# A linear-attention and MLP block on one core: key weights transposed by DMA, layernorm woven into the key loop in a fixed order, two output stages moved up

## The chip, the cores and the metric

The kernel runs on one core of a Trainium2 chip. The metric is the device time of one execution in microseconds (us); lower is better. Times of many runs are given as medians. A ratio is the mean time of one kernel's fast runs over the mean of the other's fast runs of the same rounds, so it is not quite the ratio of the medians quoted beside it; the other kernel of a ratio is always the kernel before. Positions inside an execution (start times, waits) come from the profile of one execution, whose span is some 2 us shorter than the timed run.

In the profile, PE is TensorE (matmuls), PEld its weight loads, DVE is VectorE, ACT is ScalarE, POOL is GpSimd and SPq the queue of SyncE that issues the DMA transfers. A tile is 128 of the 2048 rows; t numbers tiles from 0 to 15. The trace also records the granted clock of TensorE, which in these traces is either full or half; a stretch at half is called cold, or a half-clock window, below.

## The reference, cut to what matters

```python
# x: 1 x 2048 x 640; 32 heads of 20
def A(x):                                    # on the layernorm of x
    q, k, v = split_heads(x @ wqkv)
    pq, pk = q @ w_phi, k @ w_phi            # per head
    phi = lambda p: concat(softmax(p), softmax(-p))
    kv = phi(pk).T @ v;  z = phi(pk).sum(0)  # per head, over all rows
    return merge(phi(pq) @ kv / (phi(pq) @ z + 1e-6)) @ wo
h   = x + A(layernorm(x))
out = h + silu(layernorm(h) @ w1) @ w2
```

The sum over all rows in kv and z cuts the program in two: every key tile must have been added to the state before the first query tile can be finished.

## The kernel before

A prologue prepares weights. wv is used as loaded; the key weights wk are loaded, transposed by TensorE (wT), copied out of PSUM and multiplied with w_phi ("fold") into Wfk. Tiles 0 to 3 of the normalised x are transposed by TensorE (xT); tiles 4 to 15 go to DRAM (xs) and come back through a DMA transpose (XnT).

```python
def ln1(ts):                       # layernorm of a list of tiles, in one batch
    ...  bn_stats, bn_aggr per tile on VectorE
    ...  rstd for all of them on GpSimd
    ...  xn = (X - mean) * rstd per tile on VectorE

def stageK(t):
    ps = proj(t, Wfk)                                    # 10 matmuls
    Ek[:, 0], Ek[:, 1] = exp(ps), exp(-ps)               # ScalarE
    nc.vector.tensor_reduce(Sk, Ek, axis=X, op=add)      # row sums
    nc.vector.reciprocal(Sk, Sk)
    nc.gpsimd.tensor_tensor(Ek, Ek, Sk, op=mult)         # the multiply
# stageC(t) adds the product of Vp(t) and the normalised Ek(t) to the state in PSUM
...
with tc.manual_schedule(engines={PE, SP}):   # the scheduler orders VectorE, ScalarE, GpSimd
    for t in range(T):
        if t in (1, 5):
            ln1([t + 7, t + 8, t + 9, t + 10])
            xT_dma(t // 4 + 2)
            ...
        stageK(t)
        if t >= 4: stageV(t)
        if t >= 3: stageC(t - 3)
        ...
# later, per query tile: stageD (product with the state, division on VectorE -> o),
# stageT (transpose o), stageG (times wo, residual, second layernorm -> hn), stageTH (transpose hn),
# then stageF1 / stageF2, the MLP, in four groups of four tiles
```

The softmax here doesn't subtract the row's maximum and nothing guards it: scores larger than these inputs give would overflow.

## Time and profile before

| kernel before | |
|---|---|
| median time | 293.71 us (15 runs, 292.78 to 294.84) |
| span of the profiled execution | 291.3 us |
| busy PE / DVE / ACT / POOL | 259.6 / 141.9 / 128.8 / 72.5 us |
| mean granted TensorE clock | 0.969 |
| stageK(0) / stageC(0) / first stageD / first F1 matmul start at | 24.85 / 41.03 / 100.01 / 130.79 us |

The starts in the table, with that of stageK(5) at 46.76, cut the execution into stretches. The views of the hole before stageC(0) stand in the prediction below. One more view matters for the last part of the change, the timeline of TensorE between the first stageD and the first F1 matmul. Columns: start, length, engine, source line, operation, output and inputs, shapes, count, and in brackets how long the engine stood idle before it and what ended that.

```profile
114.21 0.28 PE L415 MATMUL mm<-ident,o 128*128 128x128 bf16 x2 [1.78 <-DVE o L404]
115.47 0.34 PE L415 MATMUL mm<-ident,o 128*128 128x128 bf16 x3 [0.97 <-DVE o L404]
...
117.06 3.56 PE L256 MATMUL mm<-XnT,Wfq 128*128 128x512 bf16 x10
```

TensorE waits twice for o, the output of stageD on VectorE, and ten Q matmuls shortly after take 3.56 us. The same ten took 2.32 us at 105.12.

### The profile page before, as it was taken

How to read it: one execution, taken by the hardware profiler on the slowest of the kernel's cores; microseconds unless marked ns; L12 is line 12 of the kernel's file. 1: busy time of each engine (PE TensorE's matmuls, PEld its weight loads, DVE VectorE, ACT ScalarE, POOL GpSimd, SP SyncE). 2: the span in 40 equal slices, each digit the busy share in tenths (PEclk: the TensorE clock that was granted, in tenths of full speed). 3: DMA queues.
4: the chain of work that ended last, by engine and by line, in shares of the span. 5: the costliest groups of instructions: out<-in, count | busy, mean ns of one | idle time of the engine just before them, and what ended most of it. 6: DMA issues, size and time to landing. Idle time of an engine off the chain costs nothing.

```text
span 291.3 us, 4919 instructions
## 1 busy us (share of the span) xinstructions
PE 259.6 (89%) x1981; PEld 169.2 (58%) x1999; DVE 141.9 (49%) x358; ACT 128.8 (44%) x189; POOL 72.5 (25%) x152
## 2 busy tenths in 40 slices
PE   6679239999999886979999999999999999999994
PEld 2456127777677454545557665556765566754672
DVE  3478784554545487662465472457354436310121
ACT  1667305777664655585551304552124543134200
POOL 6631169666455003130111101011101101100000
PEclk9979859999999999799999999999999999999999
DMA  6905788950000000000000100000110000100011
GB/s 171 400 20 154 188 222 220 406 189 1 2 0 2 0 2 0 0 3 0 2 0 0 47 23 25 0 0 3 46 47 0 2 0 23 47 23 2 0 45 46
DMA packets 20966, 17.21 MB, mean 59 GB/s; under 512 B 12304, under 2 KB 19792, under 8 KB 20944
## 3 DMA queue, kind: packets, MB, share of 16 engines
q1 hardware_dynamic: 20288, 16.88, 18.2%
q8 instruction: 15, 0.25, 0.3%
q10 hardware_dynamic: 656, 0.03, 0.2%
q14 instruction: 7, 0.06, 0.1%
HBM read 9.53 MB, written 4.59 MB: 48 GB/s over the span
## 4 chain that ended last, share of the span: by engine, by line
PE 60%; DVE 19%; ACT 7%; POOL 6%; issue 3%; DMA 3%; SPq 1%; ACTq 0%; DVEq 0%; POOLq 0%
PE mm L483 17%; PE mm L469 12%; PE mm L192 12%; PE mm L424 6%; PE mm L256 4%; PE kv L232 4%; ACT sq L435 3%; DVE u L401 3%; DMA X<-in_A_x_dram 3%; ACT EqT L261 3%; DVE stats L122 3%; DVE X L430 3%; DVE o L404 3%; POOL hm L445 2%; PE q L256 2%
## 5 line engine op out<-in xcount | busy, mean ns | idle before, releaser
L483 PE MATMUL mm<-w,shT 128*128 128x320 bf16 x448 | 63.8, 299 | 0.0
L469 PE MATMUL mm<-HnT,w 128*128 128x512 bf16 x269 | 62.4, 379 | 1.4 <-ACT HnT L460 0.8
L483 PEld LDWEIGHTS <-shT 128*128 128x128 bf16 x448 | 43.1, 98 | 16.1
L473 ACT ACTIVATE shT<-mm 128x1024 bf16<-128x1024 f32 x28 | 28.7, 1023 | 35.8 <-PE mm L469 35.8
L469 PEld LDWEIGHTS <-w 128*128 128x128 bf16 x280 | 26.7, 98 | 30.4 <-issue 0.7
L218 POOL TENSOR_TENSOR Ek<-Ek,Sk 128x1280 bf16<-128x1280 bf16 (+1 forms) x16 | 37.1, 2328 | 24.1 <-DVE Sk L216 17.5
L192 PEld LDWEIGHTS <-XnT 128*128 128x128 bf16 x320 | 31.7, 100 | 15.0 <-issue 1.7
L215 DVE TENSOR_REDUCE Sk<-Ek 128x64 f32<-128x1280 bf16 x16 | 23.5, 1481 | 25.5 <-ACT Ek L209 25.5
L430 DVE SCALAR_TENSOR_TENSOR X<-mm,X 128x640 bf16<-128x640 f32 x16 | 13.1, 821 | 44.4 <-PE mm L424 44.4
L437 POOL TENSOR_SCALAR hm<-hst 128x1 f32<-128x1 f32 x16 | 3.2, 201 | 124.4 <-DVE X L430 124.4
L490 DVE TENSOR_TENSOR ob<-mm,X 128x640 bf16<-128x640 f32 x16 | 13.2, 824 | 37.5 <-PE mm L483 37.5
L209 ACT ACTIVATE Ek<-mm 128x640 bf16<-128x640 f32 x32 | 20.8, 701 | 21.0 <-PE mm L192 20.9
L192 PE MATMUL mm<-wv,XnT 128*128 128x320 bf16 x160 | 25.2, 306 | 0.5 <-DMA wv<-in_A_wqkv_dram 0.2
L192 PE MATMUL mm<-Wfk,XnT 128*128 128x320 bf16 x160 | 25.1, 307 | 0.5 <-ACT Vp L200 0.5
L435 ACT ACTIVATE sq<-X 128x640 bf16<-128x640 bf16 x16 | 11.8, 740 | 30.5 <-DVE X L430 27.6
L424 PE MATMUL mm<-wo,ot 128*128 128x320 bf16 x160 | 24.3, 299 | 0.0
L232 PE MATMUL kv<-Vp,Ek 128*128 128x147 bf16 (+1 forms) x192 | 13.7, 224 | 10.4 <-POOL Ek L218 10.4
L460 ACT COPY HnT<-mm 128x640 bf16<-128x640 bf16 x16 | 11.1, 691 | 23.6 <-PE mm L459 23.5
L232 PEld LDWEIGHTS <-Ek 128*128 128x128 bf16 x192 | 13.4, 100 | 11.8 <-POOL Ek L218 10.7
L424 PEld LDWEIGHTS <-ot 128*128 128x128 bf16 x160 | 15.6, 98 | 7.4
L261 ACT ACTIVATE EqT<-mm 128x1024 bf16<-128x1024 f32 (+1 forms) x16 | 13.8, 914 | 12.8 <-PE mm L256 9.6
L256 PE MATMUL mm<-XnT,Wfq 128*128 128x512 bf16 x66 | 16.9, 401 | 0.8 <-ACT EqT L261 0.5
(67 smaller groups left out, 280.6 us busy)
## 6 DMA issues: line engine op xcount, KB each, us to landing
out_dram<-ob SPq DMA_DIRECT2D x16, 160.0 KB, 1.8
w<-in_B_w_dram SPq DMA_DIRECT2D x1, 2160.0 KB, 10.3
w<-in_B_w_dram SPq DMA_DIRECT2D x1, 2080.0 KB, 15.6
X<-in_A_x_dram SPq DMA_DIRECT2D x3, 640.0 KB, 10.2
xs<-xn SPq DMA_DIRECT2D x12, 160.0 KB, 2.5
wv<-in_A_wqkv_dram SPq DMA_DIRECT2D x1, 800.0 KB, 7.0
wk<-in_A_wqkv_dram SPq DMA_DIRECT2D x1, 800.0 KB, 8.6
wo<-in_A_wo_dram SPq DMA_DIRECT2D x1, 800.0 KB, 5.5
```

Of the source, the lines that this page charges most:

```text
L192: nc.tensor.matmul(ps[:, half, 0:320], xT_of(t)[:, c, :], W[:, c, half * 320 : (half + 1) * 320], start=(c == 0), stop=(c == C - 1),)
L209: nc.scalar.activation(Ek[:, s, :].rearrange("p (a n) -> p a n", a=2), ps[:, :, 0:320], AF.Exp, scale=1.0 - 2.0 * s,)
L215: nc.vector.tensor_reduce(Sk[:], Ek3, axis=AX.X, op=ALU.add)
L218: nc.gpsimd.tensor_tensor(Ek3[:, 0:n], Ek3[:, 0:n], Sk[:, 0:n].unsqueeze(2).to_broadcast([P, n, DH]), op=ALU.mult,)
L232: nc.tensor.matmul(kv[b][:, sl % 24 : sl % 24 + j1 - j0, :].rearrange("p j c -> p (j c)"), Ek[:, s, r * P : (r + 1) * P], Vp[:, HLO[r] + j ...
L256: nc.tensor.matmul(ps[:, i, :], Wfq[:, c, r * P : (r + 1) * P], XnT[g][:, c, :], start=(c == 0), stop=(c == C - 1),)
L261: nc.scalar.activation(EqT[g][:, s, rs[0] : rs[-1] + 1, :], ps[:, 0 : len(rs), :], AF.Exp, scale=1.0 - 2.0 * s,)
L424: nc.tensor.matmul(ps[:, half, 0:320], ot_of[t][:, c, :], wo[:, c, half * 320 : (half + 1) * 320], start=(c == 0), stop=(c == C - 1),)
L430: nc.vector.scalar_tensor_tensor(out=Xv, in0=ps[:, :, 0:320], scalar=1.0, in1=Xv, op0=ALU.mult, op1=ALU.add, accum_out=st[:, 0:1],)
L469: nc.tensor.matmul(ps[:, i, :], w1[:, c, fc * P : (fc + 1) * P], HnT[g][:, c, :], start=(c == 0), stop=(c == C - 1),)
L473: nc.scalar.activation(shT[g][:, 2 * k : 2 * k + 2, :], ps[:], AF.Silu)
L483: nc.tensor.matmul(ps[:, half, 0:320], shT[g][:, fc, i * P : (i + 1) * P], w2[:, fc, half * 320 : (half + 1) * 320], start=(fc == 0), stop ...
```

## The change

The intent: take the transposes of wk off TensorE and ScalarE, let the row sums of the first key tiles come before the layernorm of later tiles on VectorE, and give VectorE its output work earlier.

```diff
-    wk = first.tile([P, C, D], BF16, name="wk")          # and wT(), its TensorE transposes
-        nc.sync.dma_start(wk[:], wqkv_v[:, :, D : 2 * D])
         load_x(2, 4)
+        load_x(4, 8)
+        nc.sync.dma_start_transpose(wTk[:], A_wqkv[:, D : 2 * D])
...
+        nc.sync.dma_start_transpose(wTq[:], A_wqkv[:, 0:D])
-        for i in range(10):
+        for i in range(16):
             nc.tensor.matmul(warm_ps[:], ident[:], warm[:], start=True, stop=True)
...
-    def ln1(ts): ...
+    def ln1a(t): ...    # statistics of one tile (VectorE), rstd (GpSimd)
+    def ln1b(t): ...    # xn of one tile (VectorE)
...
         nc.vector.tensor_reduce(Sk[:], Ek3, axis=AX.X, op=ALU.add)
+        if t < 8:
+            ln1b(t + 8)
+            xs_store(t + 8)
         nc.vector.reciprocal(Sk[:], Sk[:])
...
-    with tc.manual_schedule(engines={PE, SP}):
-            if t in (1, 5):
-                ln1([t + 7, t + 8, t + 9, t + 10])
-                xT_dma(t // 4 + 2)
+    with tc.manual_schedule(engines={PE, SP, POOL, DVE, ACT}):
             stageK(t)
+            if t < 8:
+                if t < 6:
+                    ln1a(t + 10)
+                if t in (3, 7):
+                    xT_dma(t // 4 + 2)
+            if t == 8:                                   # was t == 5
+                late_loads()
+                late_consts()
...
         fill(1)
+        stageD(2)
         stageG(0)
         stageT(1)
-        stageD(2)
         fill(1)
         stageG(1)
+        stageD(3)
         stageT(2)
-        stageD(3)
```

More of the change, by code (lines that the diff above doesn't have):

```diff
@@ L14 @@
 POOL = mybir.EngineType.Pool
+DVE = mybir.EngineType.DVE
+ACT = mybir.EngineType.Activation
 BF16 = mybir.dt.bfloat16
@@ L114, with ln1a, ln1b, xs_store @@
     XnT = {}
-    def ln1(ts):
-        n = len(ts)
-        mv = sm.tile([P, n, 2], F32, name=f"mv{n}")
-        for i, t in enumerate(ts):
-            stats = sm.tile([P, 2, 6], F32, name="stats")
-            for k in range(2):
-                nc.vector.bn_stats(stats[:, k, :], X[:, t, k * 320 : (k + 1) * 320])
-            nc.vector.bn_aggr(mv[:, i, :], stats[:])
-        rstd = sm.tile([P, n], F32, name=f"rstd{n}")
-        nc.gpsimd.tensor_scalar_add(rstd[:], mv[:, :, 1], EPS)
-        nc.gpsimd.tensor_tensor(rstd[:], rstd[:], nhalf[:, 0:n], op=ALU.pow)
-        for i, t in enumerate(ts):
-            xn = first.tile([P, D], BF16, name="xn", bufs=6)
-            nc.vector.tensor_scalar(
-                out=xn[:], in0=X[:, t, :], scalar1=mv[:, i, 0:1], scalar2=rstd[:, i : i + 1],
-                op0=ALU.subtract, op1=ALU.mult,
-            )
-            xn_of[t] = xn
+    ln_of = {}
+    def ln1a(t):
+        mv = sm.tile([P, 2], F32, name="mv")
+        stats = sm.tile([P, 2, 6], F32, name="stats")
+        for k in range(2):
+            nc.vector.bn_stats(stats[:, k, :], X[:, t, k * 320 : (k + 1) * 320])
+        nc.vector.bn_aggr(mv[:], stats[:])
+        rstd = sm.tile([P, 1], F32, name="rstd")
+        nc.gpsimd.tensor_scalar_add(rstd[:], mv[:, 1:2], EPS)
+        nc.gpsimd.tensor_tensor(rstd[:], rstd[:], nhalf[:, 0:1], op=ALU.pow)
+        ln_of[t] = mv, rstd
+    def ln1b(t):
+        mv, rstd = ln_of[t]
+        xn = first.tile([P, D], BF16, name="xn", bufs=6)
+        nc.vector.tensor_scalar(
+            out=xn[:], in0=X[:, t, :], scalar1=mv[:, 0:1], scalar2=rstd[:],
+            op0=ALU.subtract, op1=ALU.mult,
+        )
+        xn_of[t] = xn
     xs = [None] + [dram.tile([GT * P, D], BF16, name=f"xs{g}") for g in range(1, G)]
+    def xs_store(t):
+        g, i = t // GT, t % GT
+        nc.sync.dma_start(xs[g][i * P : (i + 1) * P, :], xn_of[t][:])
     def xT_dma(g):
-        for t in range(g * GT, g * GT + GT):
-            i = t % GT
-            nc.sync.dma_start(xs[g][i * P : (i + 1) * P, :], xn_of[t][:])
         XnT[g] = xtp.tile([P, C, GT * P], BF16, name="XnT")
@@ L156 @@
     wts = {1: wTk, 0: wTq}
-    def wT(r):
-        ps = pools["mm"].tile([P, C, P], BF16, name="mm2")
-        for c in range(C):
-            nc.tensor.transpose(ps[:, c, :], wk[:, c, r * P : (r + 1) * P], ident[:])
-        nc.scalar.copy(wTk[:, r, :], ps[:].rearrange("p c n -> p (c n)"))
     def fold(which, ce):
@@ L263, in stageQ, with late_consts @@
             )
-    def late_loads():
+    def late_consts():
         for (s, r, j0, j1, sl) in PIECES:
@@ L270, in late_loads @@
         nc.gpsimd.memset(w2[64:128, 13, :], 0.0)
+    def late_loads():
         nc.sync.dma_start(wo[:], A_wo.rearrange("(c p) n -> p c n", p=P))
@@ L295, in masks, with phb_make @@
             )
+    def phb_make():
         nc.vector.tensor_tensor(
@@ L301, in masks @@
         )
-        for vp in Vps:
-            nc.gpsimd.memset(vp[:, :, DH : DH + 1], 1.0)
-    with tc.manual_schedule(engines={PE, SP, POOL}):
+    with tc.manual_schedule(engines={PE, SP, POOL, DVE, ACT}):
         load_x(0, 1)
@@ L308 @@
         nc.sync.dma_start(wv[:], wqkv_v[:, :, 2 * D : 3 * D])
-        nc.sync.dma_start(wk[:], wqkv_v[:, :, D : 2 * D])
         load_x(2, 4)
-        for g in range(1, G):
+        load_x(4, 8)
+        nc.sync.dma_start_transpose(wTk[:], A_wqkv[:, D : 2 * D])
+        for g in range(2, G):
             load_x(4 * g, 4 * g + 4)
+        nc.sync.dma_start_transpose(wTq[:], A_wqkv[:, 0:D])
         warm_ps = q1ps.tile([P, 512], F32, name="q1")
-        for i in range(10):
+        for i in range(16):
             nc.tensor.matmul(warm_ps[:], ident[:], warm[:], start=True, stop=True)
-        ln1([0])
-        ln1([1])
         masks()
+        ln1a(0)
+        ln1a(1)
+        ln1b(0)
         xT(0)
+        ln1b(1)
         xT(1)
         stageV(0)
-        wT(0)
         stageV(1)
-        for r in range(1, C):
-            wT(r)
-        ln1([2])
+        for vp in Vps:
+            nc.gpsimd.memset(vp[:, :, DH : DH + 1], 1.0)
+        phb_make()
+        ln1a(2)
+        ln1a(3)
+        ln1b(2)
         xT(2)
-        ln1([3])
+        ln1b(3)
+        stageV(2)
         xT(3)
         fold(1, 0)
+        stageV(3)
         fold(1, 1)
-        stageV(2)
+        ln1a(4)
+        ln1a(5)
+        ln1b(4)
+        xs_store(4)
         fold(1, 2)
+        ln1b(5)
         fold(1, 3)
-        stageV(3)
+        xs_store(5)
         fold(1, 4)
-        ln1([4, 5, 6, 7])
+        ln1a(6)
+        ln1a(7)
+        ln1b(6)
+        xs_store(6)
+        ln1b(7)
+        xs_store(7)
         xT_dma(1)
-    with tc.manual_schedule(engines={PE, SP}):
+        ln1a(8)
+        ln1a(9)
         for t in range(T):
-            if t in (1, 5):
-                ln1([t + 7, t + 8, t + 9, t + 10])
-                xT_dma(t // 4 + 2)
-                if t == 1:
-                    nc.sync.dma_start_transpose(wTq[:], A_wqkv[:, 0:D])
-                else:
-                    late_loads()
-            stageK(t)
+            stageK(t)
+            if t < 8:
[6 more added lines that the diff above has]
+                late_consts()
             if t >= GT:
@@ L362 @@
         early.close()
+    with tc.manual_schedule(engines={PE, SP}):
         pools["mm"] = ctx.enter_context(tc.tile_pool(name="mmB", bufs=4, space=PSUM))
```

## The prediction

> **What bounds the kernel now.** I read the page's strips first, then the waits of the worst stretch, the timelines of TensorE and VectorE in it, the window table, and the chain last. The strips (40 slices of 7.28 us) say where TensorE is not full:
>
> ```profile
> PE   6679239999999886979999999999999999999994
> DVE  3478784554545487662465472457354436310121
> PEclk9979859999999999799999999999999999999999
> ```
>
> TensorE is at 9 from slice 6 to the end, but for slices 13 to 16. The hole is slices 4 and 5 (29 to 44 us), where it shows 2 and 3 while VectorE shows 8 and 7, and the granted clock sinks. The timeline of TensorE there:
>
> ```profile
> 24.85 5.83 PE L192 MATMUL mm<-Wfk,XnT 128*128 128x320 bf16 x40 [0.47 <-ACT Vp L200]
> 41.03 1.25 PE L232 MATMUL kv<-Vp,Ek 128*128 128x168 bf16 x9 [10.35 <-POOL Ek L218]
> ```
>
> The four K projections (stageK 0 to 3, 40 matmuls) end at 30.68; the next work, stageC(0), must wait 10.35 us for the normalised Ek(0) from GpSimd. Why is that late? The VectorE timeline:
>
> ```profile
> 27.90 1.51 DVE L129 TENSOR_SCALAR xn<-X,mv,rstd 128x640 bf16<-128x640 bf16 x4 [1.13 <-POOL rstd L126]
> ...
> 32.03 0.21 DVE L123 BATCH_NORM_AGGREGATE mv<-stats 128x2 f32<-128x12 f32 x1
> 33.71 1.51 DVE L129 TENSOR_SCALAR xn<-X,mv,rstd 128x640 bf16<-128x640 bf16 x4 [1.47 <-POOL rstd L126]
> 35.14 2.87 DVE L215 TENSOR_REDUCE Sk<-Ek 128x64 f32<-128x1280 bf16 x2
> ```
>
> The exponentials of tile 0 were done near 27.8 (ScalarE starts them at 26.45), but VectorE first finishes the layernorm of tiles 8 to 15 in two batches of four, and starts the row sums (reduce, L215) at 35.14. So an order chosen by the scheduler, not a shortage of VectorE, makes the hole. The windows (columns: stretch, length, busy us of PE, PEld, DVE, ACT, POOL with counts, clock, DMA share, GB/s) give its size and its after-effect:
>
> ```profile
> 24.80:31.00 6.20, 5.80 (x40) 3.79 (x39) 5.07 (x17) 4.77 (x8) 1.28 (x2) 1.00 0.74 198
> 31.00:41.00 10.00, 0.00 (x0) 0.00 (x0) 8.49 (x15) 1.02 (x2) 3.64 (x4) 0.66 0.79 177
> 41.00:47.00 6.00, 5.96 (x46) 4.55 (x47) 2.17 (x4) 1.99 (x3) 6.00 (x3) 0.71 0.65 176
> 47.00:92.00 45.00, 44.83 (x419) 33.72 (x420) 22.98 (x23) 30.80 (x48) 26.83 (x12) 1.00 0.35 122
> ```
>
> From 47 us on TensorE has no holes (44.83 of 45). The chain of work that ended last agrees: layernorm on VectorE until 35.23, then
>
> ```profile
> 35.23 2.79 DVE Sk L215 x2
> ...
> 38.62 2.36 POOL Ek L218
> ...
> 41.03 1.45 PE kv L232 x12
> 42.48 3.75 PE mm L192 x20
> 46.24 0.67 PE kv L232 x12
> ```
>
> The 1.45 and 3.75 are the same work as 0.67 and 2.72 later: a cold clock costs 1.8 us more there.
>
> **What the Trainium skill says.** (1) "TensorE: Matmul & The Clock Gate", Part 1: an idle window of about 3.4 us halves the array's clock, and as much work restores it. The trace agrees: clock 0.66 in the hole, and the first ten matmuls after it take 2.54 us where later tens take 1.52. (2) The same page's opening table: VectorE, ScalarE and GpSimd run strictly in order. That is why a ready reduce stood behind layernorm work. (3) "SBUF — State Buffer", SBUF: two separate sides: VectorE operations in a two-port mode or with two SBUF inputs and GpSimd exclude each other for a whole instruction. The trace shows it once: the half-size multiply (640 columns) took 1.92 us on GpSimd beside a 0.82 us VectorE product, where half of 2.36 is 1.18. (4) "DMA: Bandwidth & Descriptors", Latency and other measured facts: 261 GB/s for a DMA transpose; this trace has 263 GB/s in a window of one (27.5 to 29.5).
>
> **The change, part by part.**
>
> *A, the wk path.* wk is no longer loaded and transposed by TensorE (25 transposes, five of 0.44 us, and five ScalarE copies of 0.69 us); wTk comes by a DMA transpose instead. On the queue it stands behind X(4..7). In before wk landed at 10.79 and wv at 8.71, so dropping wk takes 2.1 us off what follows: X(2,3) at 11.55 - 2.1 = 9.5, X(4..7) (655 KB at 414 GB/s, 1.6 us) at 11.1. wTk is 819 KB, at 263 GB/s 3.1 us, and about 1 us from last byte to semaphore: 15.2. Its issue takes 3.9 us (that of wTq did), from 3.6 to 7.5, so issue is hidden.
>
> *B, the prologue.* Sixteen warm-up matmuls end near 8 (ten took 4.45 us; I take some of the last six at full clock), which puts the first x transposes a microsecond later than in before (6.79). Then step by step, with 1.36 us for ten matmuls, 0.48 for a fold, 0.69 for a ScalarE copy and 0.15 for a handover: V(0) 9.4 to 10.7, V(1) to 12.1, T(2), V(2) 13.7 to 15.0, T(3), fold 0 at 15.4 (wTk just there), V(3) 16.6 to 17.9, folds 1 to 4 bound by the copies, ending 20.5, last copy 21.3. stageK(0) starts at 21.4 instead of 24.85: 3.5 us gained. I allow 0.5 for late wTk or a cold window: 21.9.
>
> *C, the layernorm spread over the loop; most of the gain.* VectorE's order is now fixed: reduce(t), xn(t+8), reciprocal(t), statistics(t+10). After stageK(0): matmuls 1.4, exponentials 1.3, reduce 1.45, xn 0.45, reciprocal 0.5, multiply 2.36, with handovers 7.65 us. stageC(0) starts at 29.5 instead of 41.03. The hole after stageK(3), which ends 5.6 us after stageK(0) starts, shrinks from 10.35 to 2.1, below the idle window, so the 1.8 us of cold clock mostly go too. In all at tile 5 (46.76 in before): 29.5 + 0.67 + 2.72 + 0.67 = 33.6, a gain of 13.2 us.
>
> *D, whether the loop can hold that.* VectorE per tile t < 6: reduce 1.43 + xn 0.4 + reciprocal 0.5 + statistics 0.95 = 3.3, with handovers 3.4. GpSimd: 2.36 + 0.24 + 0.58 = 3.2, with handovers 3.4. TensorE: 3.40 for t = 4, 5 and 3.71 from t = 6. All three nearly tie, so TensorE stays the bound with hardly any slack. From t = 8 both others have slack again, which absorbs the constants (about 3 us) moved onto GpSimd there.
>
> *E, the stores and transposes for tiles 8 to 15.* xn(11) is ready near 36.7, its store lands 2.5 + 0.5 us later, the transpose 5.1 us after its issue: 44.8. stageK(8) wants it at 33.6 + 3.71 x 3 = 44.7. No margin; I allow 0.5 us. Weight loads now go out near 55 and land near 70, long before use.
>
> *F, stageD(2) and stageD(3) moved up.* Between 100 and 131 us TensorE waits on VectorE's o and hn (1.78, 0.97, 1.01, 0.78 us and smaller) and runs one stretch cold (ten Q matmuls 3.56 us against 2.32). The build shows VectorE now doing tile 2's o as one block before both residual adds, where in before it stood waiting 1.22 us for hn inside it. My estimate is 1.5 us gained, plus 1 if the cold stretch goes: 2 of it taken. The four group loops after it (some 160 us) do not change.
>
> **Sum.** 13.2 (B and C) + 2 (F) - 0.5 (E) - 0.9 (GpSimd and VectorE blocking each other, or a cold window left) = 13.8; 293.3 - 13.8 = 279.5 us.
>
> **The rivals.** *R1: the wait only changes its name.* With 3.4 us tying three engines, a cadence of 4.0 (xn and the multiply excluding each other by the port rule) would make TensorE wait for Ek at every t up to 5, some 2 to 3 us, and make transpose E late by 2 more: 284. For it: the 1.92 us multiply. Against: the reduce and statistics (1.43 + 0.95) are about as long as the multiply, so xn falls into its end. *R2: the DMA transpose of wTk is late.* If transposing from the weights at queue depth, behind 2 MB of x, costs 3 us more, stageK(0) slides by the same and gain B is gone: 282 to 283. Against: wTq took 6.7 us from issue to landing with 3.9 us of that issue. *R3: all hidden, TensorE was the bound anyway.* Then 291 or more. Against: TensorE busy is 259.6 of 291.3, and the 10 us hole lies on the chain. *R4: F is worth more.* If the whole cold stretch and three waits go, 4 us: 277.
>
> **Range and chances.** R1 and R2 together give the upper end, 284.5; R4 with B in full the lower, 275.5. The 2% border is 287.5, which needs two thirds of C to fail: faster 0.94, same 0.05, slower 0.01.
>
> **What would show each step.** C: the wait of stageC on the multiply near 2 us and its start near 29.5. A and B: stageK(0) near 21.9, fold 0 not waiting for wTk for over 0.5 us. D: reduces 3.4 to 3.7 us apart for t < 6. E: no wait over 1 us before stageK(8). F: the TensorE waits for o below 2 us in sum, the cold stretch gone. If stageC(0) starts after 33, C is wrong; if it starts early and the end does not move, waits in D or E have taken its place.

## The result, and the profile after

The kernel after takes 276.53 us (12 runs, 276.04 to 278.29), the kernel before 293.71; the ratio is 0.942 (95% interval 0.940 to 0.9445). Executions over 1.5% slower than the fastest of the same kernel are left out of the means. The profiled execution spans 274.6 us at a mean clock of 0.998.

| starts at, us | before | after | gained up to here |
|---|---|---|---|
| stageK(0) | 24.85 | 20.77 | 4.08 |
| stageC(0) | 41.03 | 28.63 | 12.40 |
| stageK(5) | 46.76 | 32.73 | 14.03 |
| first stageD | 100.01 | 85.98 | 14.03 |
| first F1 matmul | 130.79 | 114.02 | 16.77 |
| end | 291.3 | 274.6 | 16.7 |

The time comes from three places and nowhere else: the prologue (4.08), the stretch from stageK(0) to stageK(5) (9.95), and the stretch from the first stageD to F1 (2.74). Between them and after them the kernels are equal to within 0.1 us. The strips of the page (40 slices, now of 6.87 us; digits are tenths of the slice) show the hole closed and the clock full:

```profile
PE   7778899999998889799999999999999999999993
DVE  4876999754446975534563733654724636200121
PEclk9999999999999999999999999999999999999999
```

The timeline of TensorE around stageC(0):

```profile
20.77 5.90 PE L191 MATMUL mm<-Wfk,XnT 128*128 128x320 bf16 x40
28.63 0.85 PE L234 MATMUL kv<-Vp,Ek 128*128 128x168 bf16 x12 [1.97 <-POOL Ek L220]
29.33 1.52 PE L191 MATMUL mm<-Wfk,XnT 128*128 128x320 bf16 x10
```

The wait for the multiply is 1.97 us where it was 10.35, and the first ten K matmuls after it take 1.52 us where they took 2.54. The timeline of VectorE tells why: the reduce now starts when the exponentials are done (2.18 us of idle before it), with layernorm work behind it instead of ahead.

```profile
23.77 1.49 DVE L214 TENSOR_REDUCE Sk<-Ek 128x64 f32<-128x1280 bf16 x1 [2.18 <-ACT Ek L208]
25.17 0.44 DVE L133 TENSOR_SCALAR xn<-X,mv,rstd 128x640 bf16<-128x640 bf16 x1
25.53 0.55 DVE L218 RECIPROCAL Sk<-Sk 128x64 f32<-128x64 f32 x1
25.99 0.82 DVE L123 BATCH_NORM_STATS2 stats<-X 128x6 f32<-128x320 bf16 x2
```

The windows from stageC(0) on and over the output stretch (length, then busy us of PE, PEld, DVE, ACT, POOL with counts, clock, DMA share, GB/s):

```profile
28.70:47.50 18.80, 18.80 (x195) 14.99 (x196) 18.63 (x34) 12.04 (x18) 18.09 (x18) 1.00 0.32 89
85.98:114.02 28.04, 23.49 (x197) 14.85 (x200) 21.20 (x71) 18.16 (x29) 5.34 (x20) 1.00 0.00 1
```

In the first, TensorE is busy all of 18.80 us, VectorE 18.63 and GpSimd 18.09: three engines tie, and TensorE loses nothing. (The busy time of VectorE includes time in which it is held up: two xn that meet the middle of a multiply, at 37.94 and 46.91, take 0.77 and 1.51 us instead of 0.44.) The second is the output stretch, 28.04 us against 30.78 before (100.01 to 130.79), with the same work. The timeline of TensorE where the kernel before ran cold now reads:

```profile
100.75 0.45 PE L482 MATMUL mm<-ident,hn 128*128 128x128 bf16 x5 [1.22 <-DVE hn L470]
101.04 2.32 PE L258 MATMUL mm<-XnT,Wfq 128*128 128x512 bf16 x10
```

The waits for o of 1.78 and 0.97 us are gone (one of 0.31 is left at 105.14), one of 1.22 for hn has grown in their place, and the ten Q matmuls run at 2.32 us. The DMA queue held one surprise. In the timeline of SPq, the issue of the new transpose takes twice as long as estimated (3.9 us), though the data arrive early (9.8 us from issue to landing by the DMA view, so at 13.0):

```profile
3.23 7.71 SPq L314 DMA_TRANSPOSE wTk<-in_A_wqkv_dram  x1
...
12.08 6.04 SPq L317 DMA_TRANSPOSE wTq<-in_A_wqkv_dram  x1
```

### The profile page after: what moved, and what is told of

The parts are those of the page before. It is cut to its first block, busy times and chain, and to the rows that moved or that the text cites. A ratio compares the mean times of both kernels' runs of the same rounds, so it can differ in the third digit from the quotient of the medians.

```text
span 274.6 us, 4884 instructions
## 1 busy us (share of the span) xinstructions
PE 254.7 (93%) x1962; PEld 166.0 (60%) x1980; DVE 144.9 (53%) x358; ACT 125.6 (46%) x184; POOL 79.0 (29%) x170
## 4 chain that ended last, share of the span: by engine, by line
PE 68%; DVE 13%; ACT 9%; POOL 5%; issue 3%; ACTq 0%; DVEq 0%; POOLq 0%
PE mm L506 18%; PE mm L191 15%; PE mm L492 13%; PE mm L447 7%; PE kv L234 4%; PE mm L258 4%; DVE u L424 3%; ACT sq L458 3%; DVE X L453 3%; DVE o L427 3%; ACT EqT L263 2%; POOL hm L468 2%; PE q L320 2%; PE q L258 2%; DVE hn L470 2%
## 5 line engine op out<-in xcount | busy, mean ns | idle before, releaser
L191 PEld LDWEIGHTS <-XnT 128*128 128x128 bf16 x320 | 30.7, 98 | 14.9 <-ACT XnT L156 2.2
L191 PE MATMUL mm<-wv,XnT 128*128 128x320 bf16 x160 | 24.2, 299 | 1.9 <-ACT XnT L156 1.9
L191 PE MATMUL mm<-Wfk,XnT 128*128 128x320 bf16 x160 | 24.1, 299 | 0.1
L483 ACT COPY HnT<-mm 128x640 bf16<-128x640 bf16 x16 | 11.1, 691 | 23.2 <-PE mm L482 22.7
L263 ACT ACTIVATE EqT<-mm 128x1024 bf16<-128x1024 f32 (+1 forms) x16 | 13.8, 914 | 12.0 <-PE mm L258 8.8
L470 DVE TENSOR_SCALAR hn<-X,hm 128x640 bf16<-128x640 bf16 x16 | 7.1, 446 | 18.3 <-POOL hm L468 18.3
L258 PE MATMUL mm<-XnT,Wfq 128*128 128x512 bf16 x66 | 15.7, 379 | 0.9 <-ACT EqT L263 0.5
L407 PEld LDWEIGHTS <-EqT 128*128 128x128 bf16 x224 | 13.7, 98 | 3.3 <-PE q L258 1.4
```

Of the source, the lines that this page charges most:

```text
L191: nc.tensor.matmul(ps[:, half, 0:320], xT_of(t)[:, c, :], W[:, c, half * 320 : (half + 1) * 320], start=(c == 0), stop=(c == C - 1),)
L258: nc.tensor.matmul(ps[:, i, :], Wfq[:, c, r * P : (r + 1) * P], XnT[g][:, c, :], start=(c == 0), stop=(c == C - 1),)
L263: nc.scalar.activation(EqT[g][:, s, rs[0] : rs[-1] + 1, :], ps[:, 0 : len(rs), :], AF.Exp, scale=1.0 - 2.0 * s,)
```

## The experiments

All ten kernels gave correct outputs. The theory: the wait before stageC(0) was an order on VectorE, costing its length and a cold clock after it; the faster prologue pays in full only once that hole is closed, and the output stages add their gain apart from both. The main rivals: the gain comes from the wk path or the reordered output stages; or the woven loop gives its gain back as waits, because three engines tie and VectorE and GpSimd exclude each other. The parts are named as in the prediction: A and B the prologue, C the layernorm in the loop, F the output stages.

### Part C alone, on the kernel before

```diff
 # kernel before, with ln1a / ln1b and stageK of after
-    with tc.manual_schedule(engines={PE, SP}):
+    with tc.manual_schedule(engines={PE, SP, POOL, DVE, ACT}):
         (loop body of after, with the transpose of wTq ahead of the loop and the weight loads at t == 8;
          wk path, 10 warm-up matmuls, order of stageD of before)
```

> The kernel before with part C alone: layernorm of tiles 8 to 15 spread over the loop in a fixed VectorE order; wk path, warm-up and order of stageD as before. My theory (the VectorE order makes the hole): stageK(0) stays near 24.85 us, stageC(0) starts 7.9 us after it, near 32.7 instead of 41.03, the wait before it is 2 us instead of 10.35, the cold 1.6 us after it go: 293.7 - 8.3 - 1.6 = 283.8 us. Rival (the hole needed the faster prologue as well, or the three engines that nearly tie in the loop give the gain back as waits): stageC(0) early but the end above 288.

Measured: 283.69 us (ratio 0.967, 0.9635 to 0.971). Timeline of TensorE:

```profile
25.86 5.83 PE L204 MATMUL mm<-Wfk,XnT 128*128 128x320 bf16 x40 [0.47 <-ACT Vp L212]
33.66 0.85 PE L247 MATMUL kv<-Vp,Ek 128*128 128x168 bf16 x12 [1.97 <-POOL Ek L233]
```

stageC(0) follows stageK(0) by 7.80 us, as expected, with the same 1.97 us wait as in the kernel after. stageK(0) itself came a microsecond later than in before (two half-clock windows lay in this run's prologue, at 9.1 and 19.4 us). Part C alone carries 9.7 us of the 17, and the loop gives nothing back: from stageK(5) to the first stageD it takes 53.25 us (37.76 to 91.01), the same as in before and after.

### Part C undone, on the kernel after

```diff
+        for t in range(8):            # all of it ahead of the first stageK
+            ln1b(t + 8); xs_store(t + 8)
+            if t < 6: ln1a(t + 10)
+            if t in (3, 7): xT_dma(t // 4 + 2)
         for t in range(T):
             stageK(t)
```

> The kernel after with part C undone: all layernorm of tiles 8 to 15 stands on VectorE ahead of the first row sum again; all else as after. My theory: the first reduce moves from 23.8 to about 32, stageC(0) from 28.6 to about 37, TensorE goes cold for about 1.6 us more: 276.5 + 8.5 + 1.6 = 286.6 us. Rival (C is worth only what it is alone, and A and F carry the rest): under 281.

Measured: 288.25 us (ratio 0.983). The first line is of VectorE's timeline, the last two of TensorE's:

```profile
33.84 1.48 DVE L214 TENSOR_REDUCE Sk<-Ek 128x64 f32<-128x1280 bf16 x1
...
38.80 1.45 PE L231 MATMUL kv<-Vp,Ek 128*128 128x168 bf16 x12 [12.26 <-POOL Ek L217]
40.10 2.83 PE L191 MATMUL mm<-Wfk,XnT 128*128 128x320 bf16 x10
```

The hole is back, longer than in before because stageK starts earlier: a prologue that is 4 us faster just waits longer. The first reduce moved to 33.84 (I had said 32) and the total rose by 11.7 us instead of 10. The order is fixed by hand here too, so it is the order, not the fixing, that closes the hole.

### Part A alone, on the kernel before

```diff
-        nc.sync.dma_start(wk[:], wqkv_v[:, :, D : 2 * D])
         load_x(2, 4)
+        load_x(4, 8)
+        nc.sync.dma_start_transpose(wTk[:], A_wqkv[:, D : 2 * D])
-        wT(r) for all r
```

> The kernel before with part A alone: wk not loaded, wTk by DMA transpose, no transposes of wk on TensorE and no copies of them; scheduler, warm-up and the rest as before. My theory: stageK(0) comes 2 to 4 us earlier, but stageC(0) still waits for the layernorm on VectorE, which only moves by what the earlier landing of tiles 2 and 3 gives, at most 2 us: 291.7 to 293 us, with the wait before stageC(0) grown to 11 us or more. Rival (gains add): 4 us, 289.6.

Measured: 290.99 us (ratio 0.994, 0.990 to 0.9975). The first two lines are of TensorE's timeline, the third of VectorE's:

```profile
26.95 5.83 PE L185 MATMUL mm<-Wfk,XnT 128*128 128x320 bf16 x40 [0.47 <-ACT Vp L193]
38.71 1.45 PE L225 MATMUL kv<-Vp,Ek 128*128 128x168 bf16 x12 [5.93 <-POOL Ek L211]
...
32.82 2.87 DVE L208 TENSOR_REDUCE Sk<-Ek 128x64 f32<-128x1280 bf16 x2
```

One half of the expectation was a miss. stageK(0) came 2.1 us later, not earlier: the scheduler, free to order VectorE, now put the statistics of tiles 2 and 3 ahead of xn(0), and the first x transpose waited 5.27 us; TensorE then ran cold up to 18.0, so twenty V matmuls took 5.13 us. So the wait before stageC(0) did not grow to 11 us or more but shrank to 5.93. The other half held: stageC(0) is set by VectorE. Its reduce moved from 35.14 to 32.82, stageC(0) from 41.03 to 38.71, the same 2.32 us, while stageK moved the other way. What feeds TensorE before the hole does not matter as long as the hole is there.

### Parts A and B undone, on the kernel after

```diff
+        nc.sync.dma_start(wk[:], wqkv_v[:, :, D : 2 * D])   # wT(0..4) back on TensorE and ScalarE
-        nc.sync.dma_start_transpose(wTk[:], A_wqkv[:, D : 2 * D])
-        for i in range(16):
+        for i in range(10):
```

> The kernel after with parts A and B undone: wk loaded and transposed by TensorE with copies on ScalarE, ten warm-up matmuls; the fixed order and stageD order of after. My theory: with the hole closed, the prologue is on the path, so all of its 4.1 us come back: stageK(0) near 24.9, 276.5 + 4.1 = 280.6 us. Rival (hidden as in A alone): 277 to 278.

Measured: three fast runs of 278.90, 280.55 and 281.84 us; the fourth, 283.17, is slow and is left out. Their median is 4.0 us over the kernel after; by the ratio (0.954, 0.950 to 0.9575, against 0.942) it is about 3.4. stageK(0) starts at 24.64, and TensorE's timeline goes on:

```profile
32.51 1.44 PE L241 MATMUL kv<-Vp,Ek 128*128 128x168 bf16 x12 [1.97 <-POOL Ek L227]
33.80 2.57 PE L198 MATMUL mm<-Wfk,XnT 128*128 128x320 bf16 x10
```

With the hole closed the prologue's 3.9 us come back in full at stageC(0) (32.51 against 28.63). This execution also fell into a half-clock window right at stageC(0), for 1.6 us more. Not every execution does: the fast runs go from 278.90 us at a mean clock of 0.999 to 281.84 at 0.985. The kernel with ten warm-up matmuls (below) has A without the six more, and a half-clock window at the same place of its prologue (8.3 to 11.7; here 8.7 to 12.1). Its stageK(0) starts at 21.40, so of the 3.87 us A is 3.24 and the six more matmuls are 0.63.

### Part F alone on the kernel before, and undone on the kernel after

```diff
         fill(1)
+        stageD(2)
         stageG(0)
         stageT(1)
-        stageD(2)                 # stageD(3) ahead of stageT(2) likewise; the second kernel is the reverse
```

> The kernel before with part F alone: stageD(2) ahead of stageG(0), stageD(3) ahead of stageT(2). My theory: nothing before 100 us changes and the stretch from the first stageD to the first F1 matmul shrinks from 30.8 us to about 28.0, as in the kernel after: 293.7 - 2.7 = 291.0 us, the cold stretch near 117 us gone. Rival (the later stretch only got shorter since the free-running clock window fell elsewhere in the kernel after): 292 to 293.5, cold stretch still there.

> The kernel after with part F undone. My theory: first stageD at 86 as in after, first F1 matmul 2.7 us later (116.7): 279.2 us, of which 1.2 us from ten Q matmuls at the cold clock if the idle before them again crosses a clock window, else 278.0. Rival (F gives nothing without the cold stretch): 276.5 to 277.

Measured: F alone 290.54 us (ratio 0.989, 0.985 to 0.993); F undone 280.08 us (ratio 0.952), 3.5 us over the kernel after. (In the profile of the second, 0.65 us of that is lost before the first stageD, 0.34 of it in a wait for XnT(2).) The stretch from the first stageD to the first F1 matmul is 28.03 us with F alone (99.52 to 127.55) and 30.79 with F undone (86.63 to 117.42), the same two lengths as in after and before. TensorE's timeline with F undone:

```profile
100.86 0.28 PE L438 MATMUL mm<-ident,o 128*128 128x128 bf16 x2 [1.80 <-DVE o L427]
...
104.26 2.97 PE L258 MATMUL mm<-XnT,Wfq 128*128 128x512 bf16 x10
```

The waits for o are back, and so is the cold stretch. F adds to the rest without interplay, and its worth is about 1.5 us of waits and 1.2 us of clock. The clock part is no accident of one execution: each of the five profiles without F (before, C alone, A alone, F undone and the filled hole below) has one half-clock window that starts between 102 and 122 us, and none of the seven with F has one there. In "C alone" it falls just behind the stretch, on the first F1 matmuls (nine take 3.44 us instead of 2.32), so the stretch alone, 29.74 us, does not show it.

### The hole of the kernel before, filled with idle matmuls

```diff
             stageK(t)
+            if t == GT - 1:
+                fill_ps = q1ps.tile([P, 512], F32, name="q1")
+                for i in range(42):
+                    nc.tensor.matmul(fill_ps[:], ident[:], warm[:], start=True, stop=True)
```

> The kernel before with 42 matmuls on zeros, read by nobody, put between stageK(3) and stageC(0), about 9 us of the 10.35 us hole: the hole's length stays, but the clock should not drop. Theory (the hole costs its length and then a cold restart): stageC(0) stays at 41 us, and the first work after it runs at the full clock, so 1.6 us are gained: 292.1 us. Rival (the slow first matmuls after the hole wait for the multiply of the next tile, not for the clock): unchanged, 293.7.

Measured: 291.59 us (ratio 0.992, 0.989 to 0.994). TensorE's timeline:

```profile
30.30 9.23 PE L352 MATMUL q<-warm,ident 128*128 128x512 bf16 x42
41.00 0.85 PE L232 MATMUL kv<-Vp,Ek 128*128 128x168 bf16 x12 [1.47 <-POOL Ek L218]
41.70 1.52 PE L192 MATMUL mm<-Wfk,XnT 128*128 128x320 bf16 x10
```

stageC(0) stays at 41.00, but the work behind it is fast at once: from stageC(0) to stageK(5) takes 4.10 us, against 5.73 in before. So 1.63 us of part C's gain is the clock, and it can be had without shortening the hole. The medians of the same rounds differ by 2.2 us; the interval of the ratio allows 1.6 to 3.3, so 1.63 lies at its lower end.

### xn moved into the middle of the multiply

```diff
 # stageK:
         nc.vector.tensor_reduce(...)
-        if t < 8: ln1b(t + 8); xs_store(t + 8)
         nc.vector.reciprocal(...)
 # loop:
                 if t < 6: ln1a(t + 10)
+                ln1b(t + 8); xs_store(t + 8)
```

> The kernel after with xn(t+8) moved behind the statistics of t+10 on VectorE, into the middle of GpSimd's multiply of the same tile instead of the end of the one before. Port theory (the two exclude each other): xn waits for the end of the multiply, its records show about 1.4 us or more instead of 0.45, VectorE's cadence for t below 6 becomes 4.6 us against TensorE's 3.4 to 3.7, stageC waits several times, and the total grows by 4 to 6 us: 280.5 to 282.5. Rival (no exclusion, R1 of the prediction was empty): cadence 3.2, 276.5 to 277.

Measured: 282.77 us (ratio 0.9615, 0.9585 to 0.9645), 6.2 us over the kernel after. One line of GpSimd's timeline, one of VectorE's, and two of TensorE's:

```profile
25.52 2.36 POOL L217 TENSOR_TENSOR Ek<-Ek,Sk 128x1280 bf16<-128x1280 bf16 x1 [2.30 <-DVE Sk L215]
...
26.27 1.79 DVE L133 TENSOR_SCALAR xn<-X,mv,rstd 128x640 bf16<-128x640 bf16 x1
...
32.59 0.84 PE L231 MATMUL kv<-Vp,Ek 128*128 128x168 bf16 x12 [0.95 <-POOL Ek L217]
...
49.21 1.53 PE L191 MATMUL mm<-Wfk,XnT 128*128 128x320 bf16 x10 [1.13 <-DMA XnT<-xs]
```

xn takes 1.79 us instead of 0.44. It ends at 28.06, which is 0.18 us behind the end of the multiply (27.88); in the kernel after, every xn that meets a multiply ends 0.17 to 0.19 us behind it too (for instance 32.00 against 31.81). VectorE's cadence is 4.66 us (reduces at 23.30, 27.98, 32.64, 37.30), stageC waits at six tiles for 6.1 us in sum (the first wait, 1.74, is the one that the kernel after has too), and XnT(2) is 1.13 us late for stageK(8). The exclusion is real; the order of the change places xn where the previous multiply is just ending.

### Ten warm-up matmuls instead of sixteen, on the kernel after

> The kernel after with ten warm-up matmuls instead of sixteen. The first x transpose waits for the warm-up in the kernel after (7.93 us), xn(0) is there at 6. Theory 1 (the six more only delay the prologue): stageK(0) 0.9 to 1.2 us earlier, 275.5 us. Theory 2 (they buy a warm clock): the kernels with ten show a half-clock window between 8 and 21 us, which costs 1 us or more in the prologue and may bring another at stageC(0): 277 to 278.5 us.

Measured in five rounds: 277.14 us, ratio 0.942 (0.9395 to 0.945), the same ratio as the kernel after. The edit is the one number. The profiled execution shows both effects. The first x transpose starts at 6.05 us instead of 7.93, but (TensorE's timeline, then the window of the same microseconds)

```profile
8.52 4.42 PE L191 MATMUL mm<-wv,XnT 128*128 128x320 bf16 x20 [0.38 <-DMA wv<-in_A_wqkv_dram]
...
8.30:11.70 3.40, 3.18 (x13) 1.74 (x13) 2.56 (x8) 0.89 (x2) 0.98 (x3) 0.50 1.22 241
```

the twenty V matmuls take 4.42 us at half clock, against 2.88 in after, and stageK(0) starts 0.6 us later than there. In the one run whose mean clock was 0.998 the time was 275.61 us, the lowest; the others had 0.991 to 0.997 and up to 278.14. In total neither theory is decided.

### A version meant to do better

```diff
         stageV(0)
-        stageV(1)
         ...
         xT(2)
+        stageV(1)
         xT(3)
-        (stageV(2), stageV(3) between the folds)
         fold(1, 0) ... fold(1, 4)
...
             stageK(t)
+            if t == GT - 1:
+                stageV(2)
+                stageV(3)
 # and the DMA transpose of wTq behind that of XnT(1)
```

> A version meant to beat the kernel after: stageV(2) and stageV(3) moved from the prologue into the 2 us hole behind stageK(3), the x transposes of tiles 2 and 3 one step earlier, the five folds in one row, the transpose of wTq behind that of XnT(1). Theory (the prologue is on the path and bound by ScalarE's copies and TensorE's order): stageK(0) near 18 instead of 20.8, stageC(0) near 26.3 instead of 28.6, then stageK(4) limited by XnT(1) near 27.1 instead of 29.5: 274 to 274.5 us. Rival (the first row sum waits for the layernorm of tiles 4 to 9 on VectorE, or a cold clock in a thinner prologue): above 275.5.

Measured in five rounds: 275.26 us, ratio 0.938 (0.935 to 0.940), against 0.942 for the kernel after; the intervals just touch, so a gain of about half a percent is likely but barely clear of noise; the profiled span is 1.3 us shorter (273.3). The time lies between what the two theories said. TensorE's timeline:

```profile
23.56 2.88 PE L191 MATMUL mm<-wv,XnT 128*128 128x320 bf16 x20
27.18 0.85 PE L234 MATMUL kv<-Vp,Ek 128*128 128x168 bf16 x12 [0.75 <-POOL Ek L220]
```

stageK(0) moved to 17.64, 3.1 us earlier, and the V projections fill most of the hole; yet stageC(0) gained only 1.45 us. The rival's first half was right: on VectorE the statistics of tiles 8 and 9 stand ahead of the first reduce (22.37), though the exponentials were done by about 20.6. It is the fault of the kernel before again, in small.

## Why the prediction was right

The direction, the mechanism and the range held; the time came out 3.0 us below the centre (276.5 against 279.5). Point by point:

- **The hole was an order on VectorE.** Shown twice: C alone gives 283.69 us, C undone 288.25. The 7.65 us from stageK(0) to stageC(0) measured 7.86, the wait of 2.1 us measured 1.97.
- **The cold clock after it cost 1.8 us.** It measured 1.63, and the filled hole shows that it is the clock.
- **Prologue.** The order of events was as worked out, including that the copies on ScalarE bound the folds. The size was off by 1.1 us: stageK(0) at 20.77 instead of 21.9. The 0.5 us allowed for a late wTk or a cold window was not used, and the other 0.6 is that stageK(0) was put behind the last copy: that copy ended at 21.38, as predicted, but the first matmuls of stageK(0) read the Wfk of earlier copies and did not wait for it. wTk landed at 13.0, not 15.2, without effect, since fold 0 started at 15.34. Its transfer did stand behind X(4..7), but the sum of times was too late. X(4..7) landed at 10.1 instead of 11.1; wv too landed 6.0 us after its issue instead of 7.0 once wk was no longer queued behind it, which suggests that queued transfers share the engines. And wTk landed 2.9 us after X(4..7), not 4.1: 11.1 was already the time of a landing, so the 1 us from last byte to semaphore was counted twice. That the issue of the transpose would take 3.9 us was wrong too (7.71), without effect, since it was hidden. What the prediction overlooked: the kernel before ran cold from 17.1 to 20.6 (clock 0.50, slice 2 of the strip), so part of the gain up to stageK(0) is clock.
- **The loop holds (D).** The reduces for t up to 5 come 3.15 to 3.48 us apart (all but one below the 3.4 to 3.7 that I had named), and TensorE is busy without a break. Rival R1 failed in this kernel, but not its mechanism: placed badly, xn brings exactly the waits that R1 described.
- **The transposes for later tiles (E).** I allowed 0.5 us for stageK(8). It did not wait; XnT(2) landed at 43.6 (issue at 38.84 and 4.8 us) and stageK(8) started at 43.88. "No margin" was right: with ten warm-up matmuls it waited 0.33 us, with F undone 0.34, with xn late 1.13.
- **The output stages (F).** 2.74 us instead of 2: all of the cold stretch went, of which I had counted half.
- **The sum.** In the profile 16.77 us against 13.8 predicted: 0.83 more from the start up to tile 5, 0.74 more from F, and 1.4 of allowances (E and the exclusion) that were not needed. The total came out near the 277 of rival R4, but not for its reason: F gave 2.74 us, not 4.
- **Slips in the text.** None of them moves the centre. R2 names wTq but means wTk, for which stageK(0) waits. R1 and R2 together add to about 287 by their own figures (279.5 + 4.5 + 3), not 284.5, so the upper end was too low for the two of them. The strip is below 9 in slices 13, 14, 15 and 17, not 13 to 16. The wait of 0.78 us ahead of F1 is for a copy on ScalarE, not for VectorE.

Rival R2 failed by measurement (wTk early), R3 by the totals. What the prediction did not see is how the parts depend on each other. Part A is worth 0.6% of the time alone, where the scheduler's order on VectorE even starts stageK later; on top of C, A and B are worth 3.4 to 4.0 us. Why the issue of a DMA transpose takes twice as long behind queued loads was not tested. It may be a wait for room in the queue: in the kernel before, the issue of a plain load of 80 KB behind the large weights took 7.57 us.

## What to carry to other kernels

When TensorE waits beside a busy engine, first ask whether that engine is short of time or only does its work in the wrong order: here the row sum that everything needed stood 7.3 us (27.8 to 35.14) behind layernorm that nobody needed yet. Fix that wait before speeding up what comes ahead of it, or the speed-up only lengthens the wait. When work of two engines that exclude each other is woven together, place the short instruction where the other's long one is just ending, and read from the trace that it does.

## What the Trainium skill lacked or had wrong

- "TensorE: Matmul & The Clock Gate", Part 1, ties the drop of the clock to an idle window of about 3.4 us, and gives no share of work below which a window counts as idle. Here the clock also dropped after windows with a good deal of work. Within a profile its changes lie multiples of 3.41 us apart (drops in the kernel before at 17.14, 34.21 and 116.13), so the windows can be laid out and the matmul time in each read. In "F alone" a window with 1.80 us of it kept the clock (6.16 to 9.57) and one with 1.77 lost it (12.99 to 16.40). In the twelve profiles every drop followed a window with 1.77 us or less, and no window with 1.80 or more brought one: about half. Matmul records can be missing and their ends are modelled, so the border is not as sharp as these two figures.
- "DMA: Bandwidth & Descriptors" gives the bandwidth of a DMA transpose, which fits (263 GB/s measured), but not how long the issue of one of this size holds the queue: 3.88 us for 800 KB with no load of x in flight (kernel before), 7.71 and 6.04 us behind loads of x. Plain loads of 640 KB issued in about half a microsecond there.
- "SBUF — State Buffer", SBUF: two separate sides, lacked nothing here. The runs agree with its lock for a whole instruction: the bf16 TENSOR_SCALAR beside a multiply ends 0.18 us behind it, and a reduce, which the page has as never contending, takes 1.43 us beside a multiply and 1.49 without.
